# Storing a router's index lists as three rows of 96 integers instead of 288 single integers

## Chip, cores and metric

The kernel runs on one core of one Trainium2 chip. The metric is the device time of one execution in microseconds (us), the median of the runs. Engines are named as the profile names them: PE (TensorE), PEld (its weight loads), DVE (VectorE), ACT (ScalarE), POOL (GpSimd) and SP (SyncE, which issues most of the DMAs).

## What is computed

Attention over 32 heads gives 2304 tokens of 512 numbers. A greedy router then hands each token to one of 8 experts, 288 tokens for each, by sorted scores; every expert is a two-layer network on its own tokens. A third part (h = x @ w_in, a gated softmax, a normalisation, @ w_out) runs on all tokens, in the order in which the experts give them out.

```python
def _moe_ref(x, w_gate, w1, w2):
    N, D = x.shape; E = w_gate.shape[1]; cap = N // E          # 2304, 512, 8, 288
    order = np.argsort(-(x @ w_gate).flatten())
    for idx in order:
        tok, e = (int(idx) // E, int(idx) % E)
        if assigned[tok] >= 0 or counts[e] >= cap: continue
        assigned[tok] = e; counts[e] += 1
    for e in range(E):
        h = np.maximum(x[assigned == e] @ w1[e], 0.0)
        out[assigned == e] = h @ w2[e]
def _moe2_ref(x, w_in, w_out, g_ln):
    h = x @ w_in; solu = h * softmax(h)
    return (((solu - mean(solu)) / sqrt(var(solu) + 1e-06)) * g_ln) @ w_out
```

## The kernel before

Attention fills the first half of the time (`attention`, lines 99 to 533). At its end SP loads the weights of the third part (`load_in`, `load_out`, lines 751 to 757) into SBUF for good. The second half is the class `Moe`; the change lies there and in the class `Router`.

`Router.phase(k)` (line 580) finds the 288 tokens of expert k. It is a generator, cut at each `yield` into short segments that alternate between DVE and PE: six rounds of compare (L607 or L612), count on PE (L619), test (`ge`, L622), sum on PE (L625) and minimum (`jm`, L628); then the chosen tokens (`sl`, L655 to L662), a prefix sum on PE (L666, L667), a slot for each token, a one-hot matrix `A` (L691, `A` for the slot within 96) and a product on PE (L695). Its result, 96 rows of 6 numbers, is copied to `idf6` (L698) and joined into `ix` (L699), the token numbers: 96 partitions of 3 integers. Slot c*96+a lies in partition a, column c. Between two phases `upd` (L712 to L725) updates the router's state.

`ix` has two uses. Three gathers on POOL (`g_row`, L773) take each one column of it and fetch 96 token rows for the expert. And `g_tab` (L770) stores it into a table `tab` in DRAM, on SP's queue:

```python
    def g_tab(s,k): s.nc.sync.dma_start(s.tab[k*CAP:(k+1)*CAP].rearrange("(c a) -> a c",a=96),s.rt.idx[k])
```

The table is read back by block of 128 tokens (`e2_ix`, L873, one integer to each partition) when the finished rows are scattered to the output (`e2_st`, L880).

An expert's weights come as eight loads of 512 KB on SP (`w_load`, L762 and L763, tile `raw`, three buffers). ACT rounds each to `wh` (`w_hi`, L766); DVE or POOL takes the rest `wl = raw - wh` in two halves (`w_lo`, L769). The gathered rows are transposed on PE (`g_tr`, L776) and split into `xh` and `xl` (L779, L781). Products: L790 (first layer, tile `cd`), L794 and L796 (its two halves `hh`, `hl`), L804 (second layer), L808 and L810 (`yh`, `yl`), then the third part: L816 (tiles `e1`), L820 to L851, transposes L856, L870.

The order of all this on the five in-order engines comes from a planner (class `Sched`, line 26), which lists every operation with an engine, an assumed duration, a priority, needs and buffers, and plays it through; the instructions are then written in that order. In `Moe.run` (line 881) `seg` chains the segments of the router, each needing the one ahead of it. The order is fixed when the kernel is built: at run time an engine waits at the head of its list.

Of the kernel before, what the change touches and what calls it, by code (L numbers as in the profile page):

```python
# [14 lines left out]
ALU = mybir.AluOpType  # L15
# [4 lines left out]
I32=DT.int32  # L20
# [5 lines left out]
class Sched:  # L26


    def __init__(s,bufs,lat=195,cold=0,begin=600.0):
        s.bufs=dict(bufs); s.lat=lat if isinstance(lat,dict) else dict.fromkeys(('X','PE','ACT','DVE','POOL','SP'),lat); s.cold=cold; s.begin=begin; s.ops=[]; s.name={}; s.free0={}  # L30
        s.same=dict(X=0,PE=0,ACT=155,DVE=128,POOL=105,SP=200)
# [504 lines left out]
I32=DT.int32  # L536
# [23 lines left out]
    c['ones']=C.tile([128,128],BF,name='onesb'); nc.vector.memset(c['ones'],1.0)  # L560
    return c
class Router:
    def __init__(s,tc,C,W,ps,L,consts):
        s.tc=tc; s.nc=nc=tc.nc; s.W=W; s.ps=ps; s.L=L; s.c=consts
        s.neg=C.tile([128,E],F32,name='neg'); nc.vector.memset(s.neg,0.0)
        s.rem=C.tile([128,E],F32,name='rem'); nc.vector.memset(s.rem,float(CAP))
        s.un=C.tile([128,NT],F32,name='un'); nc.vector.memset(s.un,1.0)
        s.asg=C.tile([128,NT,E],F32,name='asg'); nc.vector.memset(s.asg,0.0)
        s.idx={}; s.ev={}; s.rest=None
        s.A=C.tile([128,NT,128],BF,name='A'); nc.gpsimd.memset(s.A,0.0)  # L570
    def t(s,name,shape,dt=F32,bufs=2): return s.W.tile(shape,dt,name=name,bufs=bufs)
    def psum(s): return s.ps.tile([128,512],F32,name='rt',bufs=1)
# [5 lines left out]
    def phase(s,k):  # L578
# [69 lines left out]
            V.tensor_tensor(tmp,oh,s.be(f2),op=ALU.mult)  # L648
            ohf=s.t('ohf',[128,NT]); s.red(ohf,tmp,ALU.add)
        if k>0:  # L650
            tm2=s.t('tm2',[128,NT,E],bufs=1)
            V.tensor_tensor(tm2,s.asg,s.be(f2),op=ALU.mult)
            asf=s.t('asf',[128,NT]); s.red(asf,tm2,ALU.add)
        if k==0:
# [42 lines left out]
        idf=s.t('idf6',[96,6]); ix=s.t('ix',[96,3],I32,bufs=8)  # L697
        V.tensor_copy(idf,p[:96,:6])  # L698
        V.scalar_tensor_tensor(ix,idf[:,0:3],128.0,idf[:,3:6],op0=ALU.mult,op1=ALU.add)  # L699
        s.idx[k]=ix  # L700
        s.rest=None
        if not last: s.rest=(inr,key,gt,oh,f2)
    def update(s):
# [25 lines left out]
class Moe:  # L729
# [37 lines left out]
    def w_lo(s,k,i,e,j):  # L767
        nc=s.nc; hi,lo=s.wt[k,i]; raw=s.raw[k,i]; c=slice(j*512,j*512+512)
        (nc.vector if e=='V' else nc.gpsimd).tensor_tensor(lo[:,c],raw[:,c],hi[:,c].bitcast(F32),op=ALU.subtract)  # L769
    def g_tab(s,k): s.nc.sync.dma_start(s.tab[k*CAP:(k+1)*CAP].rearrange("(c a) -> a c",a=96),s.rt.idx[k])  # L770
    def g_row(s,k,c):
        x=s.xg[k,c]=s.W.tile([128,512],F32,name='h2',bufs=HB)[:96]
        s.nc.gpsimd.indirect_dma_start(out=x,out_offset=None,in_=s.x,in_offset=bass.IndirectOffsetOnAxis(ap=s.rt.idx[k][:,c:c+1],axis=0))  # L773
# [107 lines left out]
    def run(s):  # L881
# [4 lines left out]
        def op(key,eng,dur,pri,f,*a,**kw): X.op(key,eng,dur,pri+M['off'].get(key[0],0),lambda: f(*a),**kw)  # L886
# [11 lines left out]
        for k in range(E):  # L898
# [6 lines left out]
            def sg(name,eng,dur,g):  # L905
                nonlocal i
                seg(('r',k,name),eng,dur,p+ps*i,g); i+=1
# [7 lines left out]
            if k<E-1:  # L915
                for n in range(6):
                    g0=ph0 if k==0 and n==0 else ph
                    sg(('d',n),'DVE',{0:3200}.get(n,100+139+(710 if J[n]<63 else 1340)),g0)
                    sg(('p',n),'PE',480,ph); sg(('g',n),'DVE',77,ph); sg(('q',n),'PE',7,ph)
            sg('f','DVE',2541 if k<E-1 else 900,ph); sg('t','PE',60,ph); sg('s','DVE',2900,ph); sg('a','DVE',1940,ph); sg('i','PE',428,ph); sg('x','DVE',250,ph)  # L920
            ix=('r',k,'x')
            b0=S0+PER*k
            op(('wr',k),'SP',300,b0+M['wd'],s.w_reg,k,need=[('r',k,'f')])
            for i_ in range(8):
# [3 lines left out]
                e=M['lo' if k else 'lo0'][i_]  # L928
                for j in range(2):
                    op(('wl'+e,k,i_,j),'DVE' if e=='V' else 'POOL',605 if e=='V' else 1250,tn+M['wl']+j,s.w_lo,k,i_,e,j,lock=1,need=[('wh',k,i_)],free=[(('wd',k,i_),'raw')])  # L930
            op(('gt',k),'SP',480,-1e6,s.g_tab,k,need=[ix],late=1800)
            for c in range(3): op(('gr',k,c),'POOL',1038,-1e6+c,s.g_row,k,c,need=[ix]+([('cm',k-1,1,1)] if k else []),alloc=['h2'],late=7300)
            for dc in range(4):
                op(('gx',k,dc),'PE',246,b0+M['gx'],s.g_tr,k,dc,need=[('gr',k,c) for c in range(3)]+([('gx',k,0)] if dc else []),alloc=['tr'] if dc else ['tr','x'],free=[(('gr',k,c),'h2') for c in range(3)])
# [62 lines left out]
def whole(tc, q, k, v, w_gate, w1, w2, w_in, w_out, g_ln, out):  # L997
    nc = tc.nc
    if w_in.dtype == DT.int64:
        w_in, w_out = [a.bitcast(I32).rearrange("a (b t) -> a b t", t=2) for a in (w_in, w_out)]  # L1000
    with tc.tile_pool(name="dr", bufs=1, space=bass.MemoryType.DRAM) as DR, tc.tile_pool(name="c", bufs=1) as C, \
            tc.tile_pool(name="rt", bufs=2) as RT:
        xd = DR.tile([2304, 512], F32, name="xd")
        tab = DR.tile([2304], I32, name="tab")
        wst = DR.tile([2, 512, 1024], F32, name="wst")
        wso = DR.tile([2, 1024, 512], F32, name="wso")
        idf = C.tile([128, 128], F32, name="idf")
        make_identity(nc, idf)
        L = C.tile([128, 18, 8], F32, name="L")
        consts = route_consts(tc, C)  # L1010
        with tc.tile_pool(name="ps", bufs=1, space=PS) as ps, tc.tile_pool(name="ca", bufs=1) as CA:
            wg = CA.tile([128, 4, 8], F32, name="wg")
            nc.sync.dma_start(wg, w_gate.rearrange("(c p) e -> p c e", p=128))
            gs = CA.tile([128, 16], F32, name="gs")
            nc.sync.dma_start(gs[:, 0:8], g_ln.rearrange("(c p) -> p c", p=128))
            nc.gpsimd.tensor_scalar(gs[:, 8:16], gs[:, 0:8], 2.0**-52, 1.0, op0=ALU.mult, op1=ALU.mult)
            attention(tc, idf, q, k, v, xd, wg, L, ps, w_in, wst, w_out, wso, gs)
        with tc.tile_pool(name="w", bufs=2) as W, tc.tile_pool(name="ps2", bufs=1, space=PS) as ps, \
                tc.tile_pool(name="r", bufs=1) as R:
            rt = Router(tc, C, RT, ps, L, consts)  # L1020
            Moe(tc, R, W, ps, xd, w1, w2, wst, wso, out, tab, rt, idf).run()


# [26 lines left out]
```

## Time and profile before

| | before |
|---|---|
| runs (3) | 1081.42, 1083.17, 1085.08 us; median 1083.17 |
| profiled execution, its own time | 1080.1 us |
| its span, first to last instruction | 1078.0 us |
| busy: PE, DVE, ACT, POOL | 975.3 (90%), 788.0 (73%), 681.2 (63%), 626.7 (58%) us |
| mean granted TensorE clock | 0.964 |
| stores `tab<-ix` | 8, of 1.1 KB each |
| loads `raw` of expert weights | 64, of 512 KB each |

A timeline row has its start, the busy time, the engine, the line, the operation, output and input tiles and shapes; in square brackets stands how long the engine sat idle before it and what ended that. A row of stretches has the stretch, its length, the busy time of PE, PEld, DVE, ACT and POOL with the number of instructions, then the granted clock, the DMA share and GB/s. The profiled execution lasted 1080.1 us, 3.1 us under the median.

### The profile page before, as it was taken

Reading aid. Unit: us, or ns where it says so; the run is one execution under the profiler, and the core shown is the slowest. Engines: PE = TensorE matmul, PEld = TensorE weight load, DVE = VectorE, ACT = ScalarE, POOL = GpSimd, SP = SyncE. Lnnn points to the kernel's source line nnn. Section 1 sums busy time; section 2 is a strip of 40 time slices with the busy share of each in tenths; the row PEclk is TensorE's granted clock in tenths of the full one; section 3 lists DMA queues with packets and bytes.
Section 4 is the critical chain, followed back from the end, with each engine's and each line's share of the span. In section 5 each row is a group of like instructions: output and inputs, shape, how many; then the busy total and the mean of one; then the engine's idle time right before and its main releaser. Section 6 shows DMA issues by size and latency. Waiting matters only on the chain.

```text
span 1078.0 us, 26360 instructions
## 1 busy us (share of the span) xinstructions
PE 975.3 (90%) x10274; PEld 871.4 (81%) x10274; DVE 788.0 (73%) x1894; ACT 681.2 (63%) x1314; POOL 626.7 (58%) x634
## 2 busy tenths in 40 slices
PE   4889999999989999999626898999999999999997
PEld 3779988899879988899516787888888888989885
DVE  5799999888968888887567777877768775644232
ACT  3679988988979998999603252535345544556353
POOL 6689988999879999877805332331515032423111
PEclk9899999999999999999856999999999999999999
DMA  5844356344434444123395425142433324431000
GB/s 145 252 132 122 99 134 186 105 126 123 126 115 118 120 126 115 49 79 87 121 343 122 107 73 122 58 126 74 91 109 71 109 69 101 104 100 54 20 20 30
DMA packets 118316, 118.14 MB, mean 110 GB/s; under 512 B 15216, under 2 KB 93168, under 8 KB 118192
## 3 DMA queue, kind: packets, MB, share of 16 engines
q1 hardware_dynamic: 115216, 107.02, 36.9%
q0 software_dynamic: 2976, 9.44, 2.9%
q8 instruction: 81, 1.33, 0.5%
q14 instruction: 43, 0.35, 0.1%
HBM read 84.44 MB, written 17.84 MB: 95 GB/s over the span
## 4 chain that ended last, share of the span: by engine, by line
PE 65%; DVE 13%; ACT 8%; DMA 8%; issue 4%; POOL 2%; SPq 0%; POOLq 0%; DVEq 0%; ACTq 0%
PE e L816 8%; PE cd L804 7%; PE cd L790 7%; PE big L289 7%; PE e L870 6%; PE aux L257 6%; PE big L290 5%; DMA raw<-in_moe_w_dram 4%; PE acc L313 3%; PE acc L317 3%; PE acc L314 3%; ACT ph L294 2%; DVE mx L262 2%; PE rt L619 2%; DVE pl L305 1%
## 5 line engine op out<-in xcount | busy, mean ns | idle before, releaser
L304 POOL TENSOR_TENSOR pl<-pf,ph 128x576 f16<-128x576 f32 x192 | 251.1, 1325 | 38.0 <-ACT pf L299 33.5
L262 DVE TENSOR_REDUCE mx<-aux 128x1 f32<-128x384 f32 x420 | 215.5, 548 | 34.7 <-PE aux L257 24.6
L294 ACT ACTIVATE ph<-big 128x576 f16<-128x576 f32 x288 | 187.6, 660 | 49.7 <-PE big L290 47.4
L289 PE MATMUL big<-QM,K 128*128 128x288 f32 x576 | 177.0, 323 | 18.1 <-DVE pl L305 10.7
L769 POOL TENSOR_TENSOR wl<-raw,wh 128x512 fp32r<-128x512 f32 x68 | 93.8, 1402 | 157.7 <-ACT wh L766 115.7
L290 PE MATMUL big<-QLH,KHL 128*128 128x288 f32 x576 | 162.2, 297 | 0.0
L289 PEld LDWEIGHTS big<-QM,K 128*128 128x128 f32 x576 | 109.8, 191 | 27.4 <-DVE pl L305 14.8
L313 PE MATMUL acc<-VH,ph 128*128 128x65 f16 x1440 | 129.7, 197 | 0.4 <-DVE xb L325 0.3
L314 PE MATMUL acc<-VL,ph 128*128 128x64 f16 x1440 | 127.2, 195 | 0.0
L299 ACT ACTIVATE pf<-big 128x576 f32<-128x576 f32 x192 | 125.5, 663 | 1.1 <-POOL pl L304 0.9
L257 PE MATMUL aux<-KHL,QM 128*128 128x384 f32 x372 | 119.5, 371 | 6.4 <-DVE mx L262 4.1
L766 ACT ACTIVATE wh<-raw 128x1024 fp32r<-128x1024 f32 x64 | 67.5, 1054 | 81.0 <-DMA raw<-in_moe_w_dram 58.4
L313 PEld LDWEIGHTS <-ph 128*128 128x128 f16 x1440 | 96.8, 99 | 22.3 <-issue 8.1
L290 PEld LDWEIGHTS big<-QLH,KHL 128*128 128x128 f32 x576 | 110.2, 191 | 0.0
L314 PEld LDWEIGHTS <-ph 128*128 128x128 f16 x1440 | 99.7, 99 | 0.2
L317 PE MATMUL acc<-VH,pl 128*128 128x65 f16 x1440 | 91.8, 195 | 2.0 <-POOL pl L304 1.9
L305 DVE TENSOR_TENSOR pl<-big,ph 128x576 f16<-128x576 f32 x96 | 70.8, 749 | 22.7 <-ACT big L300 20.2
L790 PE MATMUL cd<-xh,wh 128*128 128x288 f32 x256 | 80.6, 315 | 1.4 <-DVE hl L796 1.4
L804 PE MATMUL cd<-hh,wh 128*128 128x288 f32 x256 | 78.7, 307 | 0.4 <-DVE yl L810 0.2
L790 PE MATMUL cd<-xl,wh 128*128 128x288 f32 x256 | 77.0, 301 | 0.0
L790 PE MATMUL cd<-xh,wl 128*128 128x288 f32 x256 | 76.8, 300 | 0.0
L804 PE MATMUL cd<-hl,wh 128*128 128x288 f32 x256 | 75.6, 296 | 0.0
(237 smaller groups left out, 2657.7 us busy)
## 6 DMA issues: line engine op xcount, KB each, us to landing
raw<-in_moe_w_dram SPq DMA_DIRECT2D x64, 512.0 KB
kt<-in_k_dram SPq DMA_DIRECT2D x32, 288.0 KB
vt<-in_v_dram SPq DMA_DIRECT2D x32, 288.0 KB
K<-KHL SPq DMA_DIRECT2D x32, 288.0 KB
qa<-in_q_dram SPq DMA_DIRECT2D x32, 256.0 KB
QM<-QLH SPq DMA_DIRECT2D x31, 144.0 KB
raw<-in_moe_w_in_dram SPq DMA_DIRECT2D x16, 256.0 KB
xd<-xb SPq DMA_DIRECT2D x4, 1024.0 KB
```

The lines of the kernel that those rows point to most:

```text
L257: nc.tensor.matmul(p[:,j,:384],QM[i][:,o:o+128],KHL[i][:,ks],start=True,stop=True)
L262: nc.vector.reduce_max(o,st[h]['pm',u][:,:len(un),:384],axis=AX.X)
L289: nc.tensor.matmul(p[:,j,:288],K1[i][:,c*128:(c+1)*128],QM[i][:,QO+j*288:QO+(j+1)*288],start=True,stop=False)
L290: nc.tensor.matmul(p[:,j,:288],KHL[i][:,c*128:(c+1)*128],QLH[i][:,j*288:(j+1)*288],start=False,stop=True)
L294: nc.scalar.activation(two(x['h']),x['p'][:,:,:288],AF.Exp,scale=0.0625)
L299: nc.scalar.activation(two(x['f']),x['p'][:,:,:288],AF.Exp,scale=0.0625)
L304: if KIND[g%len(KIND)]=='P': nc.gpsimd.tensor_tensor(x['l'],x['f'],x['h'],op=ALU.subtract)
L313: nc.tensor.matmul(acc[:,b,:],ph[:,s],VH[i][:,c],start=(c==0 and b==0),stop=False,skip_group_check=True)
L314: nc.tensor.matmul(acc[:,b,:64],ph[:,s],VL[i][:,c],start=False,stop=False,skip_group_check=True)
L317: nc.tensor.matmul(acc[:,b,:],pl[:,s],VH[i][:,c],start=False,stop=(c==NCK-1),skip_group_check=True)
L790: nc.tensor.matmul(p[:,:CAP],a[:,dc,cs],b[:,dc],start=(dc==0 and n==0),stop=(dc==3 and n==2))
L804: nc.tensor.matmul(p[:,:CAP],a[:,f],b[:,f],start=(f==0 and n==0),stop=(f==7 and n==2))
```

## The change

After `ix` the phase computes the same numbers once more as floats (`vf`, L700), transposes them on PE against the identity matrix into 3 rows of 96 (L704), and casts these to integers in a tile `row` of three partitions (L706). `g_tab` (L776 now) stores `row`, so that each partition gives 96 neighbouring integers of the table, 384 bytes. The gathers still use `ix`. The transpose and the cast are two new segments of the router's chain, `y` and `w`; the planner lets the store need `w`, and counts `x` as 340 ns instead of 250. Finally the second product `tm2` of a phase now uses the buffer of `tmp`. Lines of `Moe` and of the end of `Router` are 6 higher than before.

```diff
         V.scalar_tensor_tensor(ix,idf[:,0:3],128.0,idf[:,3:6],op0=ALU.mult,op1=ALU.add)
+        vf=s.t('vf',[96,3]); V.scalar_tensor_tensor(vf,idf[:,0:3],128.0,idf[:,3:6],op0=ALU.mult,op1=ALU.add)
         s.idx[k]=ix
+        yield
+        p=s.psum()
+        nc.tensor.transpose(p[:3,:96],vf,s.idn[:96,:96])
+        yield
+        s.row[k]=s.t('row',[3,96],I32,bufs=1); V.tensor_copy(s.row[k],p[:3,:96])
...
-            tm2=s.t('tm2',[128,NT,E],bufs=1)
+            tm2=s.t('tmp',[128,NT,E],bufs=1)
...
-    def g_tab(s,k): s.nc.sync.dma_start(s.tab[k*CAP:(k+1)*CAP].rearrange("(c a) -> a c",a=96),s.rt.idx[k])
+    def g_tab(s,k): s.nc.sync.dma_start(s.tab[k*CAP:(k+1)*CAP].rearrange("(c a) -> c a",a=96),s.rt.row[k])
...
-            sg('f','DVE',2541 if k<E-1 else 900,ph); sg('t','PE',60,ph); sg('s','DVE',2900,ph); sg('a','DVE',1940,ph); sg('i','PE',428,ph); sg('x','DVE',250,ph)
+            sg('f','DVE',2541 if k<E-1 else 900,ph); sg('t','PE',60,ph); sg('s','DVE',2900,ph); sg('a','DVE',1940,ph); sg('i','PE',428,ph); sg('x','DVE',340,ph); sg('y','PE',60,ph); sg('w','DVE',90,ph)
...
-            op(('gt',k),'SP',480,-1e6,s.g_tab,k,need=[ix],late=1800)
+            op(('gt',k),'SP',480,-1e6,s.g_tab,k,need=[('r',k,'w')],late=1800)
```

Since durations and needs change, the planner lays out the whole second half anew. Three places follow.

DVE, where phase 1 of the router begins (`rem` ends the update after phase 0; `wl` is half of a weight tile of expert 0, `Lm` to `oh` the first segment of phase 1, `ge` the first test). Before:

```order
L724 TENSOR_TENSOR rem<-rem,rt 128x8
L725 SCALAR_TENSOR_TENSOR rem<-f_11734,rem 128x8
L588 TENSOR_TENSOR Lm<-L,neg 128x144
L589 TENSOR_REDUCE best<-Lm 128x18
...
L609 TENSOR_TENSOR Lm<-Lm,wm 128x144
L610 TENSOR_TENSOR oh<-Lm,un 128x144
L769 TENSOR_TENSOR wl<-raw,wh 128x512 x2
L622 TENSOR_TENSOR ge<-rt,rem 31x8
```

Now:

```order
L730 TENSOR_TENSOR rem<-rem,rt 128x8
L731 SCALAR_TENSOR_TENSOR rem<-f_11734,rem 128x8
L775 TENSOR_TENSOR wl<-raw,wh 128x512
L588 TENSOR_TENSOR Lm<-L,neg 128x144
L589 TENSOR_REDUCE best<-Lm 128x18
...
L609 TENSOR_TENSOR Lm<-Lm,wm 128x144
L610 TENSOR_TENSOR oh<-Lm,un 128x144
L775 TENSOR_TENSOR wl<-raw,wh 128x512
L622 TENSOR_TENSOR ge<-rt,rem 31x8
```

One of the two halves of `wl` has moved ahead of the thirteen instructions of that segment.

SP at expert 2 (its first four weight loads). Before:

```order
L762 DMA raw<-in_moe_w_dram 128x4x256
L762 ISA
L762 DMA raw<-in_moe_w_dram 128x4x256
L770 DMA tab<-ix 96x3x1
L762 ISA
L762 DMA raw<-in_moe_w_dram 128x4x256
L762 ISA
L762 DMA raw<-in_moe_w_dram 128x4x256
```

Now:

```order
L768 DMA raw<-in_moe_w_dram 128x4x256
L768 ISA
L768 DMA raw<-in_moe_w_dram 128x4x256
L768 ISA
L768 DMA raw<-in_moe_w_dram 128x4x256
L776 DMA tab<-row 3x96
L768 ISA
L768 DMA raw<-in_moe_w_dram 128x4x256
```

The store comes one weight load later; at experts 0 and 1 it stands between the second and the third load, as before.

PE at the end of phase 1, now (before, the L804 products, L810 now, followed L695 without a break):

```order
L695 LDWEIGHTS A
L695 MATMUL rt<-Bv,A 128x6
L810 MATMUL cd<-hh,wh 128x288
L810 MATMUL cd<-hl,wh 128x288
L810 MATMUL cd<-hh,wl 128x288
L810 MATMUL cd<-hh,wh 128x288
L810 MATMUL cd<-hl,wh 128x288
L810 MATMUL cd<-hh,wl 128x288
L704 MATMUL rt<-idf,vf 3x96
L810 MATMUL cd<-hh,wh 128x288
```

Six products lie between the end of L695 and the new transpose.

## Rows read from the trace of the kernel before

**Rows 1.** Stretches of the second half (stretch, length, engines, clock, DMA, GB/s)

```profile
580.00:700.00 120.00, 107.65 (x914) 95.90 (x914) 92.75 (x254) 46.85 (x87) 42.53 (x36) 0.94 0.38 89
700.00:860.00 160.00, 158.13 (x1217) 138.37 (x1216) 119.03 (x354) 75.67 (x142) 50.60 (x50) 1.00 0.39 95
860.00:1020.00 160.00, 157.22 (x1026) 139.72 (x1025) 82.12 (x213) 75.71 (x141) 51.36 (x53) 1.00 0.29 78
```

**Rows 2.** Timeline of PE, the three longest waits between 580 and 700

```profile
620.21 0.16 PE L625 MATMUL rt<-ge,ms 31*128 31x8 bf16 x1 [2.20 <-DVE ge L622]
...
648.07 0.18 PE L666 MATMUL rt<-sl,tri 128*128 128x36 bf16 x1 [2.39 <-DVE sl L661]
...
670.93 0.16 PE L625 MATMUL rt<-ge,ms 31*128 31x8 bf16 x1 [2.95 <-DVE ge L622]
```

**Rows 3.** Timelines of DVE and of ACT at the first and last of these

```profile
619.04 0.46 DVE L810 TENSOR_TENSOR yl<-cd,yh 128x288 fp32r<-128x288 f32 x1 [2.86 <-ACT yh L808]
...
617.65 1.06 ACT L766 ACTIVATE wh<-raw 128x1024 fp32r<-128x1024 f32 x1 [6.88 <-DMA raw<-in_moe_w_dram]
...
668.98 1.06 ACT L766 ACTIVATE wh<-raw 128x1024 fp32r<-128x1024 f32 x1 [6.25 <-DMA raw<-in_moe_w_dram]
```

**Rows 4.** Timeline of SP, stores and the loads behind them

```profile
606.50 4.80 SPq L762 DMA_DIRECT2D raw<-in_moe_w_dram  x2
...
657.79 0.34 SPq L770 DMA_DIRECT2D tab<-ix  x1
658.38 1.00 SPq L762 DMA_DIRECT2D raw<-in_moe_w_dram  x2
...
703.29 0.35 SPq L873 DMA_DIRECT2D ixb<-tab  x1
...
921.01 0.34 SPq L770 DMA_DIRECT2D tab<-ix  x1
```

**Rows 5.** Stretches behind a store, and one behind a table read (703 to 709)

```profile
658.00:661.00 3.00, 3.00 (x24) 2.93 (x24) 1.90 (x10) 2.75 (x6) 2.34 (x3) 1.00 0.85 5
661.00:666.00 5.00, 4.56 (x48) 4.42 (x47) 4.35 (x18) 0.41 (x1) 0.54 (x1) 1.00 0.46 41
703.00:709.00 6.00, 6.00 (x39) 5.48 (x38) 5.62 (x21) 4.87 (x8) 3.21 (x4) 1.00 0.90 300
921.00:926.00 5.00, 5.00 (x38) 4.86 (x37) 3.96 (x11) 2.30 (x6) 0.00 (x0) 1.00 0.38 12
```

**Rows 6.** Gathers of token rows, the tile's answer: issue to landing

```profile
DMA to landing us min/median/max: 5.4/10.2/12.3
```

**Rows 7.** Stretches behind the waits at 620 and 671: the clock

```profile
621.20:624.60 3.40, 3.40 (x28) 2.49 (x27) 2.73 (x6) 0.74 (x2) 0.00 (x0) 0.50 0.55 159
672.40:675.80 3.40, 3.40 (x27) 2.72 (x26) 2.90 (x7) 2.41 (x3) 0.04 (x1) 0.50 0.92 238
```

**Rows 8.** Nearest operations to the added ones: by line, tile and timeline

```profile
L271 PE MATMUL aux<-identr,mr x32: 218/225/308, 23.0 to 506.6; 128*5 128x128 f32 x32
...
L274 DVE CAST mt<-aux 5x128 fp32r<-5x128 f32 x32 | 8.8, 274 | 2.4 <-PE aux L271 2.1
...
L699 DVE SCALAR_TENSOR_TENSOR ix<-idf x8: 158/158/570, 558.1 to 920.8; 96x3 int32<-96x3 f32 x8
...
542.82 0.17 DVE L628 TENSOR_REDUCE jm<-rt 128x1 f32<-128x8 f32 x1 [0.25 <-PE rt L625]
```

**Rows 9.** Timelines of DVE, ACT and PE at the start of expert 0

```profile
559.70 0.30 DVE L588 TENSOR_TENSOR Lm<-L,neg 128x144 f32<-128x144 f32 x1
...
566.33 1.06 ACT L766 ACTIVATE wh<-raw 128x1024 fp32r<-128x1024 f32 x1 [2.26 <-DMA raw<-in_moe_w_dram]
...
567.48 1.29 DVE L769 TENSOR_TENSOR wl<-raw,wh 128x512 fp32r<-128x512 f32 x2 [4.63 <-DMA raw<-in_moe_w_dram]
...
568.89 0.16 PE L625 MATMUL rt<-ge,ms 31*128 31x8 bf16 x1 [5.37 <-DVE ge L622]
...
575.32 0.90 PE L776 MATMUL tr<-idf,h 96*128 96x96 f32 x4 [1.45 <-DMA h<-xd,ix]
```

More of the change, by code (lines that the diff above doesn't have):

```diff
@@ L562, with __init__ @@
 class Router:
-    def __init__(s,tc,C,W,ps,L,consts):
-        s.tc=tc; s.nc=nc=tc.nc; s.W=W; s.ps=ps; s.L=L; s.c=consts
+    def __init__(s,tc,C,W,ps,L,consts,idn):
+        s.idn=idn; s.tc=tc; s.nc=nc=tc.nc; s.W=W; s.ps=ps; s.L=L; s.c=consts
         s.neg=C.tile([128,E],F32,name='neg'); nc.vector.memset(s.neg,0.0)
@@ L568, in __init__ @@
         s.asg=C.tile([128,NT,E],F32,name='asg'); nc.vector.memset(s.asg,0.0)
-        s.idx={}; s.ev={}; s.rest=None
+        s.idx={}; s.row={}; s.ev={}; s.rest=None
         s.A=C.tile([128,NT,128],BF,name='A'); nc.gpsimd.memset(s.A,0.0)
@@ L1019, in whole @@
                 tc.tile_pool(name="r", bufs=1) as R:
-            rt = Router(tc, C, RT, ps, L, consts)
+            rt = Router(tc, C, RT, ps, L, consts, idf)
             Moe(tc, R, W, ps, xd, w1, w2, wst, wso, out, tab, rt, idf).run()
```

## Prediction

> **What bounds the kernel now.** I read the stretches of the second half first, since the change touches nothing before it. From 700 to 1020 us PE is busy for 158.13 of 160 and 157.22 of 160 us [rows 1]: there it is the bound, and an earlier table, an earlier gather or an earlier weight load buys nothing. Between 580 and 700 it is busy for 107.65 of 120 us [rows 1], so 12.35 us are idle. Whatever is won there moves all later work forward, because PE then has a full list to the end.
>
> Next come PE's waits in that stretch. The three longest are 2.20, 2.39 and 2.95 us [rows 2]. The reader should follow the first one back. PE waits for the router's test `ge` on DVE; DVE stood 2.86 us at `yl` (L810), waiting for ACT's copy of `yh`; and ACT stood 6.88 us at a rounding `wh`, waiting for a weight load [rows 3]. The last one has the same cause, with 6.25 us on ACT [rows 3]. The middle one waits for the router's own arithmetic on DVE.
>
> Then SP's queue and the DMA rates. The load that ACT awaits at 617.65 was issued at 606.50, the one awaited at 668.98 at 658.38: 11.15 and 10.6 us for 512 KB. The second stands right behind the store of the index list, issued at 657.79 [rows 3, 4]. From 658 to 661 the DMA engines moved 5 GB/s, from 661 to 666 41 GB/s, though a weight load and three gathers were waiting [rows 5]. Two other rows tell what did it. At 921.01 the store is again followed by almost nothing, 12 GB/s over 5 us [rows 4, 5], and there no gather is under way. At 703.29 a read of the table, 128 single integers, is followed by 300 GB/s [rows 4, 5]. So it is the store of 288 single integers that holds up the transfers behind it, for some 5 to 8 us; neither short reads nor gathers do.
>
> **The change, part by part.** *The store.* 288 elements of 4 bytes become three rows of 384 bytes. If the hold-up goes, a load issued at 607 needs 1.7 us for its 512 KB at 300 GB/s [rows 5], and twice that beside gathers of 590 KB; it is there well before 615, even if the store waits 1 us longer for `row`. The waits of 2.20 and 2.95 us then have no cause: 5.15 us [rows 2]. Each is followed by a stretch of 3.40 us in which PE is busy throughout at a granted clock of 0.50, its lower level of 1.2 GHz [rows 7]; without the idle time ahead of them I count these at full speed, which gives back half of each, 1.7 us twice. Together **-8.55 us**. At expert 2 the third load even stands ahead of the store now. The gathers, 10.2 us in the median and 5.4 at best [rows 6], should come nearer to the latter, but after 700 nothing waits for them.
>
> *New work on PE.* Eight transposes; the nearest row, 128x5, takes 0.225 us [rows 8]. The one of phase 0 falls into PE's idle time, seven count: **+1.6**. Bounds are 0 (they fill waits) and 1.6.
>
> *New work on DVE and in the router's chain.* `vf` costs 0.16 as `ix` does, the cast 0.27 as L274 does, with two hand-overs of 0.25 and the transpose of 0.225 between [rows 8]: 1.15 us more for each phase. The DVE work itself, 0.43 us eight times, hides beside PE. Queued behind the cast on DVE is the update and the next phase; behind the store on SP wait weight loads that had 5 us of hold-up before. In front of PE stands L704: from the end of L695 until `vf` is there take two hand-overs and three small instructions, 1.0 us. With six products between, I take 0.25 for phases 1 and 2 and nothing later, where nine or more products stand between: **+0.5**. For the later start of the next phase's rounds I take another **+0.5**: bounds are 0 and seven times 1.15, 8 us, and PE had other work in nearly every place, so it lies near the lower one. The shared buffer of `tmp` costs nothing, since the same engine ran both products one after the other anyway.
>
> *The new order at expert 0.* Half of `wl` now stands ahead of phase 1's first segment. Before, that segment began at 559.70, and PE had its counts done 5.37 us ahead of 568.89, at 563.5: 3.8 us. Then all waited for `wl`, whose load landed at 566.33 [rows 9]. Now the segment starts only after landing, rounding (1.06) and half a `wl` (0.65), so PE's L625 comes about 6.2 us after the landing instead of at 568.89. If the load still lands at 566.33, that is 3.6 us later. ACT's idle 2.26 and its rounding of 1.06 before show that the load ahead was in by 563.0; 512 KB more at 300 GB/s are in by 564.7, some of it earlier: 0.8 to 2.0 us later. Against that, PE waited 1.45 us for gathered rows at 575.32 [rows 9], which now land sooner. Bounds -1.5 and +3.6; I take **+1.5**, nearest to the row of the landing.
>
> Sum: -8.55 + 1.6 + 0.5 + 0.5 + 1.5 = -4.45 us. The profiled execution lasted 1080.1 us, so its like would last 1075.6; from the median of 1083.17 the forecast is **1078.7 us**.
>
> **A rule against the change.** The rows say that 288 short writes hold up the queue; no row shows writes of 384 bytes in three partitions to DRAM from this queue beside weight loads. The Trainium skill, "DMA: Bandwidth & Descriptors", asks for at least 512 bytes for the full rate and says that shorter ones are read, modified and written back (Specifications); it also warns that an outermost dimension of less than 16 confines a DMA to so many engines (Rules for kernel authors). By that rule the new store would still be of the slow kind, and on three engines instead of sixteen; this is the first rival below. The trace has no run that separates length from number.
>
> **The rivals.** *The hold-up stays*, because it belongs to any short write and not to their number: then only the costs are left, 1.6 + 0.5 + 0.5 + 1.5 = 4.1, and the time is 1087.3. For it: the stretch after a store is slow beyond the moment of the store itself, 41 GB/s over 5 us [rows 5]. Against it: three pieces of work instead of 288. Chance 0.10.
>
> *PE waits at L704 in every phase* (slower). PE takes its list in order, so if DVE is late with `idf6` and `vf`, behind halves of `wl` or `yl`, all products behind the transpose stand. The price of such a wait is at most like the one at 648.07, 2.39 us [rows 2]. With s us in each of seven phases the sum is -8.55 + 1.6 + 0.5 + 1.5 + 7s; it passes zero at s = 0.7. At half of 2.39, 1.2 us, it is +3.4: 1086.6. For it: PE does wait for the router's DVE work now. Against it: from 700 on such waits sum to less than 5 us in 320 [rows 1]. Chance 0.11.
>
> *The waits only move.* PE is let go at 618 and 668, but the next test or the next weight half is late instead, and half of the 8.55 is lost again: 1083.0. For it: the router's DVE chain was the cause at 648. Chance 0.12.
>
> *More is won.* The new order happens to lose the wait of 2.39 too, and expert 0 starts no later: -4.45 - 2.39 - 1.5, or 1074.8. Chance 0.15.
>
> **How the numbers follow.** The forecast has a chance of 0.52, with an own range of 1075.2 (expert 0 starts 1.5 us sooner, plus half a us) to 1080.8 (it starts 3.6 us later). About 0.3%, 3.2 us, is what a measurement of this kernel tells from no change: faster means below 1079.9. Three quarters of the forecast's chance lie there, 0.39, and with the better case it is 0.54. The hold-up that stays and the waits at L704 give 0.21 for slower. The rest, 0.25, is no change. The range goes down to 1071.5: the better case with expert 0 at -1.5, and a half-clock stretch of 1.7 saved with the wait of 2.39. It goes up to 1087.5, to hold both slower cases at their prices; beyond lie some 0.15.
>
> **What would show it.** Right: behind each store the DMA rate at once near 300 GB/s; weight loads landing 3 to 5 us after issue; ACT's 6 us waits for loads at experts 1 and 2 gone, and with them PE's two waits and the stretches of half clock; gathers near 5.4 us; eight transposes of about 0.2 us at L704 with waits of less than 0.3 us before them; PE's first product of expert 0 some 1 us later. Wrong, if the rate behind a store stays below 50 GB/s, if PE waits at L704 or elsewhere between 580 and 700 for 12 us as before, or if the idle time after 700 grows by more than 4 us.

## The result and the profile after

| | before | after |
|---|---|---|
| median of the runs (4 each) | 1082.89 us | 1073.64 us |
| lowest and highest | 1081.42, 1085.08 | 1072.38, 1074.12 |
| profiled execution, its own time | 1080.1 | 1074.12 |
| its span | 1078.0 | 1072.3 |
| mean granted TensorE clock | 0.964 | 0.961 |

The ratio is 0.9911, with a 95% interval from 0.9892 to 0.993: 9.25 us faster, where 4.45 were forecast. A later comparison on another chip, below, gives 4.93 us for the same two kernels. Both figures have to be explained.

The stretches of the changed kernel's second half (stretch, length, busy time of PE, PEld, DVE, ACT, POOL, then clock, DMA share, GB/s), which answer to [rows 1]:

```profile
580.00:700.00 120.00, 112.80 (x932) 99.81 (x932) 86.20 (x247) 47.57 (x88) 39.28 (x35) 0.96 0.31 93
700.00:860.00 160.00, 157.71 (x1249) 138.08 (x1245) 128.16 (x371) 75.74 (x143) 56.65 (x53) 1.00 0.31 94
860.00:1020.00 160.00, 157.59 (x1022) 141.11 (x1023) 82.73 (x220) 77.62 (x146) 48.87 (x53) 1.00 0.25 76
```

PE's idle time between 580 and 700 fell from 12.35 to 7.20 us. Behind 700 it stayed: 4.65 us before, 4.70 now.

Next the stretches behind two stores (issued at 658.26 and 916.62), which answer to [rows 5], and the two stretches of half clock that are left between 590 and 700, which answer to [rows 7]:

```profile
658.00:661.00 3.00, 3.00 (x16) 2.29 (x15) 2.93 (x14) 2.78 (x6) 2.49 (x4) 1.00 0.68 192
661.00:666.00 5.00, 2.92 (x29) 2.41 (x28) 4.90 (x19) 1.29 (x3) 1.38 (x1) 0.88 0.79 252
917.00:922.00 5.00, 5.00 (x35) 4.72 (x35) 3.27 (x9) 2.44 (x5) 0.00 (x0) 1.00 0.66 192
600.00:603.40 3.40, 3.40 (x16) 3.40 (x16) 3.19 (x12) 0.00 (x0) 0.00 (x0) 0.50 0.58 196
664.90:668.30 3.40, 3.40 (x24) 3.11 (x20) 1.90 (x6) 0.00 (x0) 0.03 (x1) 0.51 0.36 119
```

192 and 252 GB/s stand where 5, 41 and 12 stood: the hold-up behind the store is gone. The gathers say the same; the answer of their line, against [rows 6]:

```profile
DMA to landing us min/median/max: 4.6/5.7/6.7
```

Four of PE's waits between 590 and 700, the two longest among them, from its timeline, against [rows 2]:

```profile
598.14 0.18 PE L666 MATMUL rt<-sl,tri 128*128 128x36 bf16 x1 [1.64 <-DVE sl L661]
...
607.70 0.24 PE L704 MATMUL rt<-idf,vf 96*3 96x96 f32 x1 [0.47 <-DVE vf L700]
...
647.09 0.18 PE L666 MATMUL rt<-sl,tri 128*128 128x36 bf16 x1 [0.77 <-DVE sl L661]
...
664.57 0.60 PE L619 MATMUL rt<-oh,cmp 128*31 128x8 bf16 x18 [2.08 <-DVE oh L610]
```

Both waits for `ge` behind a late weight load are gone, and the wait for `sl` shrank from 2.39 to 0.77. Two others came with the new order: 1.64 us for `sl` of phase 1 and 2.08 us for `oh` of phase 3, each with a stretch of half clock behind it in this trace. They stand in place of two shorter ones in the order of before:

```profile
605.10 0.38 PE L695 MATMUL rt<-Bv,A 128*128 128x6 bf16 x9 [1.43 <-DVE A L691]
...
613.31 0.59 PE L619 MATMUL rt<-oh,cmp 128*31 128x8 bf16 x18 [1.22 <-DVE oh L610]
```

ACT's timeline shows both sides: the load at expert 1 now lands in time, and one at expert 2, issued late, has 3.06 us of waiting before it, against 6.88 and 6.25 in [rows 3].

```profile
612.71 1.06 ACT L772 ACTIVATE wh<-raw 128x1024 fp32r<-128x1024 f32 x1 [0.21 <-DMA raw<-in_moe_w_dram]
...
650.07 1.06 ACT L772 ACTIVATE wh<-raw 128x1024 fp32r<-128x1024 f32 x1 [3.06 <-DMA raw<-in_moe_w_dram]
```

Last, the start of expert 0, which answers to [rows 9], from the timeline of all engines:

```profile
563.20 0.69 DVE L775 TENSOR_TENSOR wl<-raw,wh 128x512 fp32r<-128x512 f32 x1 [5.02 <-POOL wl L775]
...
563.80 0.30 DVE L588 TENSOR_TENSOR Lm<-L,neg 128x144 f32<-128x144 f32 x1
...
566.88 4.82 DVE L775 TENSOR_TENSOR wl<-raw,wh 128x512 fp32r<-128x512 f32 x1
567.02 0.62 PE L619 MATMUL rt<-oh,cmp 128*31 128x8 bf16 x18 [9.49 <-DVE oh L610]
...
567.44 3.70 POOL L775 TENSOR_TENSOR wl<-raw,wh 128x512 fp32r<-128x512 f32 x3
...
571.82 0.16 PE L625 MATMUL rt<-ge,ms 31*128 31x8 bf16 x1 [4.19 <-DVE ge L622]
```

DVE stands 5.02 us until the half of `wl` that was put ahead of phase 1's first segment can run, and PE stands 9.49 us. Then the other half takes 4.82 us instead of 0.69, while POOL runs three halves of its own beside it.

### The profile page after: what moved, and what is told of

It is laid out like the page before. It is cut to its first block, busy times and chain, and to the rows that moved or that the text cites. A ratio compares the mean times of both kernels' runs of the same rounds, so it can differ in the third digit from the quotient of the medians.

```text
span 1072.3 us, 26389 instructions
## 1 busy us (share of the span) xinstructions
PE 975.3 (91%) x10282; PEld 871.5 (81%) x10282; DVE 790.8 (74%) x1910; ACT 681.1 (64%) x1314; POOL 627.7 (59%) x634
## 4 chain that ended last, share of the span: by engine, by line
PE 66%; DVE 16%; ACT 8%; issue 4%; DMA 3%; POOL 1%; SPq 0%; POOLq 0%; DVEq 0%; ACTq 0%
PE cd L810 10%; PE e L822 9%; PE e L876 7%; PE big L289 6%; PE cd L796 6%; PE aux L257 5%; PE big L290 5%; PE acc L313 3%; PE acc L317 3%; PE acc L314 3%; DVE mx L262 3%; ACT ph L294 2%; PE rt L619 2%; ACT big L300 1%; DVE pl L305 1%
## 5 line engine op out<-in xcount | busy, mean ns | idle before, releaser
L775 POOL TENSOR_TENSOR wl<-raw,wh 128x512 fp32r<-128x512 f32 x68 | 96.2, 1438 | 150.9 <-ACT wh L772 104.1
L810 PE MATMUL cd<-hh,wh 128*128 128x288 f32 x256 | 80.7, 315 | 0.9 <-DVE hl L802 0.7
L810 PE MATMUL cd<-hl,wh 128*128 128x288 f32 x256 | 76.8, 300 | 0.0
L810 PE MATMUL cd<-hh,wl 128*128 128x288 f32 x256 | 76.7, 300 | 0.0
```

The costliest lines, as they stand in the source:

```text
L810: nc.tensor.matmul(p[:,:CAP],a[:,f],b[:,f],start=(f==0 and n==0),stop=(f==7 and n==2))
```

## The experiments

Twelve runs in three groups of four, each group on one chip with the kernel before beside it: 1083.39, 1077.0 and 1078.92 us there. Ratios are therefore compared within a group.

### First group: the store's form and the order, apart

**The kernel before, once more.** No edit.

> The kernel before, once more, for a second trace and for the noise. Both theories: ratio 1.000 within 0.2%, about 1083 us. In its trace the stretch 580 to 700 has some 12 us of PE idle again, with the two waits of 2 to 3 us behind a weight load that follows a store. Should its attention part be as much as 2.5 us longer or shorter than in the first trace, then that much of a difference between two single traces is no work of the change.

Measured: 1082.59 us, ratio 1.0 [0.9976, 1.0023], from 1078.56 to 1086.48 in ten runs. Its profiled run lasted 1084.27 us, against 1080.1 for the one that the prediction read, and its waits for `ge` are longer than in [rows 2]:

```profile
621.11 0.16 PE L625 MATMUL rt<-ge,ms 31*128 31x8 bf16 x1 [3.24 <-DVE ge L622]
...
672.66 0.16 PE L625 MATMUL rt<-ge,ms 31*128 31x8 bf16 x1 [4.19 <-DVE ge L622]
```

3.24 and 4.19 us for 2.20 and 2.95. PE also waits for gathered rows behind 700, 2.29 us in sum against 0.41 in the first trace. The longest of these:

```profile
732.28 0.55 PE L776 MATMUL tr<-idf,h 96*128 96x96 f32 x4 [0.89 <-DMA h<-xd,ix]
...
843.48 0.55 PE L776 MATMUL tr<-idf,h 96*128 96x96 f32 x4 [0.41 <-DMA h<-xd,ix]
...
908.10 0.55 PE L776 MATMUL tr<-idf,h 96*128 96x96 f32 x4 [0.51 <-DMA h<-xd,ix]
```

Of these two executions the longer one is that in which more time is lost to late loads and gathers.

**The new order with the old store.** The changed kernel, transposes and all, but the table is filled from `ix`:

```diff
-    ...rearrange("(c a) -> c a",a=96),s.rt.row[k])
+    ...rearrange("(c a) -> a c",a=96),s.rt.idx[k])
```

> The changed kernel with its order of instructions, its transposes and casts, but the store again as 288 single integers of ix. Theory A (288 short writes hold up the transfers queued behind them, the order matters little): the gain goes, 1081 to 1084 us, about 8 us above the changed kernel, with a DMA rate of under 50 GB/s for 5 us behind each store and gathers landing after 10 us. Theory B (the newly planned order made the gain): 1073 to 1075 us, like the changed kernel.

Measured: 1086.09 us, ratio 1.0037 [1.0017, 1.0057], above what either theory expected. The hold-up is back (stretch behind the store at 661.32). At expert 1 PE stands 4.32 us where `yh` is late, because ACT had waited 8.49 us for a weight load:

```profile
661.50:669.50 8.00, 5.99 (x27) 4.53 (x27) 6.83 (x28) 5.31 (x10) 4.65 (x6) 1.00 0.49 34
```

```profile
618.65 1.06 ACT L772 ACTIVATE wh<-raw 128x1024 fp32r<-128x1024 f32 x1 [8.49 <-DMA raw<-in_moe_w_dram]
...
620.06 0.79 PE L822 MATMUL e<-winh,yh 128*128 128x512 f32 x1 [4.32 <-ACT yh L814]
```

So the new order and its new work, beside the old store, cost 2.7 us; all of the gain comes from the store.

**The old order with three rows.** The order of before on PE; `row` is made on DVE from a counter instead of from the index list, so the rows of the output go to other places; `tm2` shares the buffer of `tmp` as in the changed kernel:

```diff
-        s.idx[k]=ix
+        s.idx[k]=ix; row=s.row[k]=s.t('row',[3,96],I32,bufs=1)
+        V.tensor_scalar(row,s.row0,1.0,float(k*CAP),op0=ALU.mult,op1=ALU.add)
+        V.tensor_scalar(row[0:1,0:1],ix[0:1,0:1],0.0,float(k*CAP),op0=ALU.mult,op1=ALU.add)
...
-    ...rearrange("(c a) -> a c",a=96),s.rt.idx[k])
+    ...rearrange("(c a) -> c a",a=96),s.rt.row[k])
```

> The order of the kernel before, without transposes; the store writes three rows of 96 integers made by two small DVE instructions from a counter, not the index list, so the table is simply the slots in order and the finished rows go to the wrong places; all transfers have the changed kernel's sizes. Theory A: 1072 to 1075 us, as the 8.55 us of waits and half-clock stretches go and expert 0 does not start later, so a little below the changed kernel. Theory B: 1082 to 1084 us, like the kernel before.

Measured: 1066.31 us, ratio 0.9851 [0.9823, 0.9879], some 6 us below the range of theory A. In the 8 us behind the store at 646.56 the rate is 205 GB/s:

```profile
646.80:654.80 8.00, 8.00 (x75) 7.74 (x74) 7.09 (x31) 5.31 (x10) 2.61 (x3) 1.00 0.72 205
```

On this chip the store's form is worth 17.1 us in the order of before, twice the 8.55 us that were counted. The changed kernel, which isn't in this group, had 9.25 us in the first comparison, about half of that.

**Triples.** The order of before exactly and no new instruction: slot 3a+c instead of 96c+a, so that a partition's three integers are neighbours in the table, 96 pieces of 12 bytes. The transposes of the gathered rows write every third column instead:

```diff
-    ...rearrange("(c a) -> a c",a=96),s.rt.idx[k])
+    ...rearrange("(a c) -> a c",a=96),s.rt.idx[k])
...
-  s.nc.tensor.transpose(p[:,c*96:(c+1)*96],...)
+  s.nc.tensor.transpose(p[:,:CAP].rearrange('p (a c) -> p c a',c=3)[:,c],...)
```

> The order of the kernel before; slots are numbered a*3+c instead of c*96+a, so ix is stored as 96 pieces of 12 bytes without transpose or cast, and the gathered rows are transposed into every third column. Theory A in the form that the number of writes counts, 288 for some 7 us: 96 hold up for a third, 2 to 2.5 us, and the loads are still in time: 1072 to 1076 us. Theory A in the form that any store of pieces of a few bytes holds up alike, or Theory B: 1082 to 1084 us. If writing every third column of PSUM slows the gather's transposes from 0.246 us, that shows in their rows.

Measured: 1066.64 us, ratio 0.9849 [0.9824, 0.9875], below both kernels and below the range expected. The gathers' transposes take 0.246 us in the median as before. Two stretches behind the store at 650.58, and that from 580 to 700:

```profile
650.80:653.80 3.00, 3.00 (x24) 2.92 (x24) 2.18 (x13) 2.73 (x6) 2.36 (x3) 1.00 0.66 5
653.80:658.80 5.00, 5.00 (x52) 4.81 (x51) 4.66 (x17) 1.77 (x3) 0.52 (x1) 1.00 0.90 281
...
580.00:700.00 120.00, 113.35 (x966) 101.10 (x965) 98.74 (x285) 52.45 (x95) 45.85 (x39) 0.98 0.36 101
```

The 3 us at 5 GB/s are as in [rows 5], but then the rate is full: a third of the pieces, less than half of the hold-up, and what is left of it costs nothing that can be measured beside the kernel with three rows (1066.31 us).

### Second group: what the hold-up is, and the two parts of the new order

**Spread.** The kernel before with the table's integers 512 bytes apart in DRAM. The store is still 288 writes of 4 bytes:

```diff
-        tab = DR.tile([2304], I32, name="tab")
+        tab = DR.tile([2304, 128], I32, name="tab")
...
-    ...s.tab[k*CAP:(k+1)*CAP].rearrange("(c a) -> a c",a=96)...
+    ...s.tab[k*CAP:(k+1)*CAP,0].rearrange("(c a) -> a c",a=96)...
```

The read of the table (L873) takes the same places.

> The kernel before, with the table's integers 512 bytes apart in DRAM: the same 288 writes of 4 bytes for each store, but no two to neighbouring addresses. If the number of writes is what holds up the transfers: 1081 to 1085 us, as the kernel before. If it is that many writes fall into the same few hundred bytes: 1066 to 1070 us, with gathers landing in 5 to 6 us and no slow stretch behind a store.

Measured: 1065.67 us, ratio 0.9894 [0.9871, 0.9917]. Behind its store at 650.35:

```profile
650.60:658.60 8.00, 8.00 (x75) 7.74 (x74) 7.01 (x30) 4.59 (x9) 2.88 (x3) 1.00 0.71 202
```

As many writes, as short, and no hold-up: 202 GB/s over 8 us. So neither their number nor their length alone holds up the transfers; it takes that they go to neighbouring bytes.

**Double.** Each store made twice, the second into a table of its own that nobody reads:

```diff
-    def g_tab(s,k): s.nc.sync.dma_start(s.tab[k*CAP:(k+1)*CAP]...)
+    def g_tab(s,k):
+        for t in (s.tab,s.tab2): s.nc.sync.dma_start(t[k*CAP:(k+1)*CAP]...)
```

> The kernel before, with each store of 288 integers made twice, the second into a table that nobody reads. If the hold-up grows with the number of writes: loads and gathers behind a store land some 6 us later again, and the waits at experts 0, 1 and 2 grow by 3 to 6 us each: 1092 to 1101 us. If a store holds up the queue once, whatever its number: 1083 to 1086 us.

Measured: 1080.02 us, ratio 1.0024 [1.0008, 1.0039]. Behind the pair at 655.63:

```profile
655.80:658.80 3.00, 3.00 (x25) 2.93 (x24) 2.17 (x13) 2.76 (x6) 2.30 (x3) 1.00 1.13 27
658.80:663.80 5.00, 5.00 (x52) 4.81 (x51) 4.52 (x16) 0.41 (x1) 0.57 (x1) 1.00 0.68 33
```

27 and 33 GB/s, much as after one store. Twice the writes to two regions hold up hardly longer than once: the expectation of a doubling was wrong. That fits "spread", where the place of the writes counts and not their number, but doesn't show it; doubling within one region wasn't tried.

**The transposes alone.** The new instructions and the three rows, but written inside the segment `x`, so that the order of before stays:

```diff
+        vf=s.t('vf',[96,3]); V.scalar_tensor_tensor(vf,idf[:,0:3],128.0,idf[:,3:6],...)
+        p=s.psum()
+        nc.tensor.transpose(p[:3,:96],vf,s.idn[:96,:96])
+        s.row[k]=s.t('row',[3,96],I32,bufs=1); V.tensor_copy(s.row[k],p[:3,:96])
```

> The changed kernel's transposes, casts and three rows, but issued at the place where the kernel before makes ix, without segments of their own, so that all engines keep the order of the kernel before. If the transposes and their hand-overs are cheap and the newly planned order is what costs: 1067 to 1070 us, that is 1066.5 for rows in the old order plus 1.6 us of PE work and up to 2 us of waits. If the transposes themselves make PE wait (about 1 us in each of seven phases): 1073 to 1075 us.

Measured: 1069.03 us, ratio 0.992 [0.9895, 0.9946], its runs from 1065.39 to 1072.09. Against "spread" beside it, which has none of the new instructions, it is 3.4 us more; the two intervals overlap, so the size of that is uncertain. The traces, below, say about the same.

**The half of `wl` back in its place.** The changed kernel, with one more need in the planner that keeps the half behind phase 1's first segment on DVE:

```diff
-  ...need=[('wh',k,i_)],...
+  ...need=[('wh',k,i_)]+([('r',1,('d',0))] if k==0 and e=='V' and i_==1 else []),...
```

> The changed kernel, but the half of wl that stood ahead of phase 1's first segment on DVE is kept behind that segment; all else is planned as in the changed kernel. In the traces expert 0's first product came 43.8 us after the router's first in the changed kernel and 38.5 us after it in the kernel of triples. If this one displacement is what the new order costs: 1068 to 1071 us, with that distance at 39 to 41 us. If the cost lies in the rest of the new order or in the transposes: 1073 to 1074 us, as the changed kernel.

Measured: 1070.52 us, ratio 0.9947 [0.9927, 0.9968]. The changed kernel isn't in this group; the third sets the two side by side.

### Third group: the changed kernel beside its variants

**The changed kernel, once more.** No edit.

> The changed kernel once more, beside three others on the same chip, since the earlier runs of it were made beside none of the experiments. Theory A (the hold-up behind the store is gone, and the new order gives part of that back): ratio 0.989 to 0.993 against the kernel before, as at first. Theory B (half of its gain was the difference between chips): 0.995 to 1.0. The first product of expert 0 comes 43 to 45 us after the router's first count.

Measured: 1073.99 us (1072.71 to 1074.67), ratio 0.9954 [0.9938, 0.9969] against 1078.92 for the kernel before. The changed kernel takes the same time as at first, 1073.64; it is the kernel before that is 4 us faster on this chip. That is theory B for the size: about half of the 9.25 us goes with how long the kernel before takes where it runs. The other half, 4.93 us, is clear of the noise.

**The half of `wl` in its place, beside it.** The edit as above.

> The changed kernel with the half of wl kept behind phase 1's first segment on DVE, on the same chip as the changed kernel. Theory A (the half of wl costs expert 0 some 5 us, and PE has a full list later): 3 to 5 us faster than the changed kernel beside it. Theory B (the later part of the new order waits for something else anyhow, so an earlier expert 0 only lengthens later waits): within 2 us of the changed kernel.

Measured: 1070.34 us (1069.12 to 1070.73), ratio 0.9918 [0.9901, 0.9935]: 3.65 us faster than the changed kernel, as theory A had it. Its DVE and PE at expert 0, in the timeline:

```profile
560.18 0.62 PE L619 MATMUL rt<-oh,cmp 128*31 128x8 bf16 x18 [3.78 <-DVE oh L610]
...
563.56 0.16 PE L625 MATMUL rt<-ge,ms 31*128 31x8 bf16 x1 [2.76 <-DVE ge L622]
...
566.27 5.45 DVE L612 SCALAR_TENSOR_TENSOR A<-key,jm,thr 128x1134 bf16<-128x1134 f32 x1
566.81 3.71 POOL L775 TENSOR_TENSOR wl<-raw,wh 128x512 fp32r<-128x512 f32 x3
```

PE's wait before L619 is 3.78 us instead of 9.49. The long DVE instruction beside POOL's three halves is still there in this trace, 5.45 us, but now it is a later one; in the trace of the second group it isn't (last section).

**Spread, once more.** The edit as above.

> The kernel before with the table's integers 512 bytes apart, on the same chip as the next one. Theory A (the store's form in the old order is worth 1.1 to 1.5%): ratio 0.985 to 0.990 against the kernel before. Theory B (the earlier figure was the scatter of one chip): 0.992 or more.

Measured: 1068.54 us, ratio 0.9904 [0.9884, 0.9924]: 10.4 us, close to theory A's upper end and short of B's range, though the interval reaches into both.

**Spread, but not at expert 0.** Expert 0's integers go side by side into a small table of their own:

```diff
-    ...s.tab[k*CAP:(k+1)*CAP,0].rearrange("(c a) -> a c",a=96)...
+    ...(s.tab0 if k==0 else s.tab[k*CAP:(k+1)*CAP,0]).rearrange("(c a) -> a c",a=96)...
```

The table is read back from both; one block of 128 tokens takes two reads.

> As the one before, but expert 0's 288 integers are stored side by side as in the kernel before, so that the hold-up is back at expert 0 alone. The prediction counted nothing for expert 0's hold-up. Theory A (half of the gain that the prediction missed lies there: gathers and weight loads of expert 0 come later and the whole list moves): 3 to 6 us slower than the one before, and the first product of expert 0 some 2 to 3 us later. Theory B (the hold-up at expert 0 is hidden, as the prediction took it): within 1.5 us of the one before, and the whole gain lies at experts 1 and 2.

Measured: 1069.82 us, ratio 0.9921 [0.9903, 0.9938], 1.3 us more than the one before it (the intervals overlap), and in the traces the first product of expert 0 comes 0.6 us later, counted from the router's first count (table below): theory B. The stretch from 5.6 us behind expert 0's store (up to then some 290 to 390 GB/s are moved), first with neighbouring integers and then spread (its times are 2 us earlier):

```profile
562.00:569.00 7.00, 0.97 (x20) 0.65 (x19) 3.25 (x9) 3.17 (x3) 5.06 (x4) 0.50 0.64 43
```

```profile
560.00:567.00 7.00, 1.21 (x21) 0.83 (x20) 3.88 (x9) 2.52 (x3) 5.71 (x5) 0.50 0.44 116
```

The hold-up is there, 43 GB/s, and in this pair little waits for it. Most of the gain lies behind expert 0, where the prediction counted it; how much lies at expert 0 isn't settled, as the table below shows.

## Why the prediction was right in direction and half in size

Attention runs ahead of the change, and its length differs from run to run: the router's first count on PE (L619) starts anywhere from 531.7 to 537.3 us. So the traces are split at that count and at the first product of expert 0 (L790 in the kernel before), with the start of the last product (L870) as the end; other kernels have the same lines up to 6 higher:

| kernel | first count | expert 0 | last | count to expert 0 | expert 0 to last |
|---|---|---|---|---|---|
| before | 536.8 | 578.3 | 1071.1 | 41.5 | 492.8 |
| before, once more | 537.3 | 578.1 | 1075.3 | 40.8 | 497.2 |
| double | 535.5 | 575.8 | 1072.1 | 40.3 | 496.3 |
| new order, old store | 531.7 | 577.1 | 1074.0 | 45.4 | 496.9 |
| after | 534.3 | 578.2 | 1065.4 | 43.9 | 487.2 |
| after, again | 537.1 | 580.4 | 1065.7 | 43.3 | 485.3 |
| `wl` in its place | 535.4 | 573.7 | 1061.8 | 38.3 | 488.1 |
| the same, again | 533.2 | 573.8 | 1061.8 | 40.6 | 488.0 |
| transposes alone | 536.7 | 575.4 | 1062.3 | 38.7 | 486.9 |
| three rows, old order | 532.8 | 570.9 | 1054.2 | 38.1 | 483.3 |
| spread | 536.2 | 574.7 | 1058.7 | 38.5 | 484.0 |
| spread, again | 532.9 | 573.5 | 1057.2 | 40.6 | 483.7 |
| spread but 0 | 534.9 | 576.1 | 1059.6 | 41.2 | 483.5 |
| triples | 536.4 | 574.8 | 1058.1 | 38.4 | 483.3 |

These five stretches go from the first product of expert 0 to the last product: the kernel before, "spread, again", the changed kernel twice, and the transposes alone. The first number behind the length is PE's busy time.

```profile
578.30:1071.10 492.80, 474.52 (x3404) 416.54 (x3403) 312.70 (x866) 224.74 (x419) 151.60 (x150) 0.98 0.32 80
573.50:1057.20 483.70, 471.18 (x3404) 414.42 (x3402) 312.57 (x866) 224.72 (x419) 151.00 (x150) 0.99 0.27 82
578.20:1065.40 487.20, 474.01 (x3409) 416.48 (x3408) 314.68 (x879) 223.80 (x418) 152.04 (x150) 0.99 0.27 81
580.40:1065.70 485.30, 472.31 (x3409) 414.78 (x3409) 314.41 (x879) 223.72 (x418) 151.92 (x150) 0.99 0.27 82
575.40:1062.30 486.90, 473.08 (x3412) 414.90 (x3410) 314.42 (x880) 225.26 (x419) 151.09 (x150) 0.99 0.27 82
```

**The store, -8.55: right against the trace that it was read from.** Behind expert 0's first product "spread, again" is 9.1 us shorter than before. Of these, 5.76 us are PE's idle time (18.28 before, 12.52 then) and 3.34 its busy time, where the term had 5.15 of waits and 3.4 of half clock. The two long waits for `ge` and the half clock behind them went; the wait for `sl` and its half clock stayed, as the term had it:

```profile
639.57 0.18 PE L666 MATMUL rt<-sl,tri 128*128 128x36 bf16 x1 [2.39 <-DVE sl L661]
```

**The base of the forecast: this step failed.** The step "from the median of 1083.17 the forecast is 1078.7 us" carried the sum over from a run of 1080.1 us, as if the 3.1 us between the two had nothing to do with the change. The runs say that much of it had. The kernel before, once more, needs 4.4 us longer behind expert 0 (497.2 for 492.8). Its waits for `ge` at L625 are 2.3 us longer in sum and its waits for gathered rows behind 700 1.9 us; for the latter the prediction had "after 700 nothing waits for them". All four traces with 288 single integers side by side at every store need 492.8 to 497.2 us behind expert 0, and the one that was read is the shortest of them. In the old order with no hold-up behind experts 1 and 2 and no new instructions on PE the same stretch takes 483.3 to 484.0 us in five traces from three chips; and the changed kernel takes 1073.64 and 1073.99 us where the kernel before takes 1082.89 and 1078.92. Set against the execution that was read, the sum gave 1075.6, 1.6 to 2.0 above what came. From the first count to the end that execution takes 534.3 us and the two traces of the changed kernel 531.1 and 528.6: 3.2 and 5.7 less, with the 4.45 of the sum between them. So the -8.55 holds for that execution; in one of 1084 us the same hold-up costs some 4 us more, and the change takes those away too. That rests on one pair of traces and on the medians. Not all scatter is the hold-up's: the runs of "three rows, old order" go from 1063.05 to 1068.75 us without it. Why the hold-up costs more in one execution, or on one chip, than in another is open.

**Expert 0, +1.5: too small.** The count to expert 0 takes 43.3 and 43.9 us against 41.5 and 40.8 before, 1.8 to 3.1 more. The term assumed that only the landing, a rounding and 0.65 us of `wl` stand ahead. It left out that the other half would run beside POOL's three halves and take 4.82 us, as it does in both traces of the changed kernel. Back in its place, the half of `wl` gives 38.3 and 40.6. By the medians that is worth 3.65 us; by these traces 2.7 to 5.6 us of it come ahead of expert 0 and 0.8 to 2.8 are lost again behind. In the pair of the third group they cancel, 528.6 us from count to end in both, and the rest of that pair's difference stands ahead of the router; where the 3.65 us lie is not settled by them.

The hold-up behind expert 0's own store stands in the sum only as earlier gathers. The table says that it may be more. Without it (or with the short one of "triples"), five traces with the half of `wl` behind the segment take 38.1 to 38.7 us; with it, four take 40.3 to 41.5. Two without it take 40.6: those in which L612, a compare of the router on DVE, takes 5.46 and 5.45 us beside POOL (last section). The trace of "spread but 0", 41.2, has such an L612 too. So from 0.6 to some 3 us may lie there, by which executions are compared.

**New work, waits at L704 and later rounds, +2.6: about right.** From expert 0 on, the changed kernel needs 485.3 and 487.2 us against 483.7 for "spread, again", 1.6 to 3.5 more. By the stretches above, 0.5 and 0.7 us of this are idle time of PE and 1.1 and 2.8 busy time. The transposes take 0.244 us each, by the answer of line L704, as supposed, and seven of them 1.7 us:

```profile
L704 PE MATMUL rt<-idf,vf x8: 242/244/318, 556.1 to 916.1; 96*3 96x96 f32 x8
```

PE waits for `vf` twice in eight phases, 0.61 (in phase 0) and 0.47 us, so the rival of a wait at L704 in every phase fell. The new waits for `sl` and `oh`, 1.64 and 2.08 us, are no loss beside "spread": the order of before has waits for `A`, `oh` and `sl` in their place, and the idle time is nearly the same. So the rival that the waits only move fell too. The second trace of the changed kernel has 1.7 us less of busy time than the first; it has the same wait for `oh`, but full clock behind it:

```profile
666.16 0.59 PE L619 MATMUL rt<-oh,cmp 128*31 128x8 bf16 x18 [2.10 <-DVE oh L610]
...
666.60:670.00 3.40, 3.40 (x30) 3.19 (x27) 3.08 (x10) 0.00 (x0) 0.00 (x0) 1.00 0.37 124
```

The transposes alone, in the order of before, need 486.9 us. So this cost goes with the new instructions and not with the new order; what the order costs stands ahead of expert 0, 43.3 and 43.9 us against 38.7.

**The rule against the change fell.** Three rows of 384 bytes, each below 512, on at most three partitions, are followed by 192 and 252 GB/s, and 288 writes of 4 bytes in "spread" by 202. The rule of the Trainium skill, "DMA: Bandwidth & Descriptors" (Specifications), that transfers below 512 bytes are read, modified and written back may hold, but a slow queue doesn't follow from it in this kernel.

**In sum**, on the chip of the third group: the store's form -10.4, the new order with its work +5.45 (4.1 counted), together -4.93 us. A forecast of -4.45 fits there. The 9.25 us of the first comparison are these and the 4 us by which the kernel before takes longer where that was made. Their 1073.64 us lie below the forecast's own range (from 1075.2) and nearest to the rival "more is won", 1074.8, but its mechanism didn't come: expert 0 starts later, and the wait for `sl` that shrank has others beside it.

## What to carry to other kernels

When a change removes a wait whose length varies, the part of the median above the profiled run can be part of that wait: set the forecast from the run that was read, and look whether the slow runs are slow by the same wait. A store of about 1 KB that is scattered in pieces of 4 bytes over one short piece of DRAM can hold up the transfers issued behind it; order the slots so that each partition's elements are neighbours, or lay them out apart, before any instruction is added to pack them. And where an order comes from a planner, price the order by itself: here it and the new instructions together gave back half of what the store had won.

## What the runs showed of the hardware

What holds up the queue is short writes into neighbouring bytes of DRAM. This row is the kernel before, the 8 us behind its store at expert 2:

```profile
658.00:666.00 8.00, 7.56 (x70) 7.34 (x70) 6.25 (x28) 3.16 (x7) 2.88 (x3) 1.00 0.61 28
```

So 288 of 4 bytes side by side: 28 GB/s over 8 us; 96 of 12 bytes side by side: 3 us at 5 GB/s, then full rate; three rows of 384 bytes, or 288 of 4 bytes at a distance of 512: no hold-up. What happens in the memory or on the way there isn't shown by these profiles.

The second is DVE beside POOL. A half of `wl` takes 0.69 us on DVE and 4.82 us when it starts 0.56 us ahead of three halves on POOL (567.44, 3.70 us); it ends 0.56 us after the last of them. The Trainium skill, "SBUF — State Buffer" (Who interferes with whom), says that a VectorE instruction with two inputs in SBUF and a GpSimd instruction that reads SBUF contend for a shared pair of ports, an exclusive lock, and that the loser is blocked for the whole instruction. The rows agree, but for one thing: DVE is shown as having started first, and lost to three instructions in a row. In the changed kernel with the half of `wl` in its place the same befalls L612, 5.45 us beside POOL's 3.71, in the trace of the third group. In that of the second, DVE wins, and POOL takes 1 us longer instead:

```profile
567.97 1.40 DVE L612 SCALAR_TENSOR_TENSOR A<-key,jm,thr 128x1134 bf16<-128x1134 f32 x1
568.67 4.73 POOL L775 TENSOR_TENSOR wl<-raw,wh 128x512 fp32r<-128x512 f32 x3
```

So one kernel has both outcomes. In the traces read for it, DVE lost where it is shown 0.53 to 0.56 us ahead of POOL (five times) and won where it is shown 0.70 or 0.71 us ahead (four times); what lies between, and why, isn't shown.
